# A second level of Strassen in the gate and value products of three of four segments

## The chip, the cores and the metric

The kernel runs on one core of a Trainium2 chip. The metric is device time in microseconds of one execution. Before the change the median was 796.1 us (794.5 to 797.4, three runs). Engines are named as the profile names them: PE is TensorE's matmuls, PEld its weight loads, DVE is VectorE, ACT ScalarE, POOL GpSimd, SPq the sequencer that issues most DMAs.

## The reference

A recurrent retention layer (batch 4, 8 heads, 768 positions, head size 64), whose output is turned into 3072 rows of 512, goes into a gated feed-forward block with 1536 hidden units. q, k, v and the output are fp32; the three weights arrive as fp64, and the kernel turns them into fp32 in segment 1, so all products are fp32.

```python
for t in range(S):
    state = gamma * state + outer(k[t], v[t])      # per head
    y[t] = scale * q[t] @ state
x = y.transpose(0, 2, 1, 3).reshape(3072, 512)
g = x @ w_gate
out = (g * sigmoid(g) * (x @ w_val)) @ w_out
```

## The kernel before

The 3072 rows are worked on in four segments. A segment has three stages: retention in chunks of 128 positions; **up**, the gate and value products for twelve blocks of hidden units; **down**, the product with `w_out` for three row tiles, between whose products the next segment's retention is slipped in. Up and down each use one level of Strassen-Winograd: seven products in place of eight. One block of up:

```python
def up(s, f, convert):
    ...
    def product(o, slot, a, start=True, stop=True):
        for k in range(KH):                        # KH = 2
            nc.tensor.matmul(o, w[:, slot, k], a[:, k], ...)   # 128 x 384
    product(x, B11, a_up(0, 0))
    p1 = tmp("p1", 2); nc.scalar.copy(p1, x)
    product(wb, T1, s1)
    p5 = tmp("p5", 1); nc.scalar.copy(p5, wb)
    product(x, T2, s2, start=False)                # accumulates onto x
    u2 = tmp("u2", 1); nc.scalar.copy(u2, x)
    product(wb, B22, s4, start=False)
    tt(hT[:, f, 0], wb, u2, op=add)                # VectorE
    ...                                            # three more products
    def muls():                                    # a block later
        tt(hT[:, f, 0], hT[:, f, 0], c11, op=mul)
        tt(hT[:, f, 1], hT[:, f, 1], sg, op=mul)
```

The seven operand blocks of a weight (four blocks and three differences) are made in segment 1 and kept in HBM for the later segments. In down, VectorE also makes four sums of the hidden activations per row tile (`sum_h`, 768 elements a partition).

## Time and profile before

I cut the span at the first and last matmul of each stage. In the last column stands the time in which PE neither streams nor overlaps, counted as steps between matmul starts that are over 0.15 us longer than the columns need.

| Stage | us | PE gaps, us |
|---|---|---|
| retention of segment 1 | 37.1 | (waits for its first loads) |
| up 1 | 130.4 | 21 |
| down 1 | 80.8 | 2.2 |
| up 2, up 3, up 4 | 108.4 each | 0 |
| down 2 | 78.4 | 0 |
| down 3 | 79.3 | 0.7 |
| down 4 | 54.2 | 0 |

### The profile page before, as it was taken

What the parts mean: (1) busy time and instruction counts of PE and PEld (TensorE: products, weight loads), DVE (VectorE), ACT (ScalarE), POOL (GpSimd) and SP (SyncE); (2) the same over time, 40 slices, a digit from 0 to 9 for tenths busy, and PEclk for the clock granted to TensorE, in tenths of its full rate; (3) what the DMA queues carried; (4) which work ended last, traced back from release to release, by engine and by line L of the source; (5) the groups of instructions that cost most, each with busy time, mean ns of one, the idle gap of its engine ahead of it and who ended that gap; (6) DMA issues with size and microseconds to landing.
All of it is one profiled execution on the core that took longest, in us unless ns stands there. A gap on an engine that the chain in (4) does not pass through costs nothing.

```text
span 794.6 us, 8792 instructions
## 1 busy us (share of the span) xinstructions
PE 758.9 (96%) x3440; PEld 532.4 (67%) x3440; DVE 333.4 (42%) x524; ACT 202.4 (25%) x422; POOL 138.2 (17%) x102
## 2 busy tenths in 40 slices
PE   5889888989999999999999999999999999999997
PEld 4755454557888555557888655556888755555886
DVE  2778888885241232225441322225433222223520
ACT  2374454411211222221122222322111122322100
POOL 3665766732110000100211000001211000000000
PEclk9899999999999999999999999999999999999999
DMA  9856667331550223500532223320254023310010
GB/s 328 287 199 232 203 220 250 148 120 54 186 195 31 93 92 99 192 0 28 199 118 108 73 93 113 128 97 14 67 212 159 27 93 113 119 47 0 1 54 26
DMA packets 40840, 95.73 MB, mean 120 GB/s; under 512 B 3680, under 2 KB 15968, under 8 KB 40800
## 3 DMA queue, kind: packets, MB, share of 16 engines
q1 hardware_dynamic: 37344, 88.89, 32.1%
q10 hardware_dynamic: 3456, 6.29, 2.3%
q8 instruction: 27, 0.44, 0.2%
q14 instruction: 13, 0.11, 0.0%
HBM read 77.86 MB, written 17.30 MB: 120 GB/s over the span
## 4 chain that ended last, share of the span: by engine, by line
PE 77%; DVE 3%; issue 0%; ACT 0%; DVEq 0%; ACTq 0%
PE x L349 24%; PE dx L417 15%; PE w L349 12%; PE dw L417 7%; PE z L349 6%; PE dz L417 4%; PE y L296 2%; PE s L246 2%; PE y L292 2%; PE st L274 2%; DVE hs L407 1%; DVE hT L390 0%; DVE a L251 0%; DVE hT L372 0%; DVE wot L201 0%
## 5 line engine op out<-in xcount | busy, mean ns | idle before, releaser
L349 PE MATMUL x<-xT,wt 128*128 128x384 f32 x384 | 136.3, 497 | 13.9 <-DVE hT L372 13.9
L349 PE MATMUL x<-xs,wt 128*128 128x384 f32 x384 | 139.8, 487 | 1.2 <-ACT u L368 1.2
L349 PE MATMUL w<-xs,wt 128*128 128x384 f32 x384 | 139.6, 486 | 0.9 <-DVE xs L334 0.9
L349 PEld LDWEIGHTS x<-xT,wt 128*128 128x128 f32 x384 | 73.8, 194 | 67.6 <-issue 20.8
L370 DVE TENSOR_TENSOR hT<-w,u 128x384 f32<-128x384 f32 x48 | 26.7, 557 | 214.0 <-PE w L349 213.1
L349 PEld LDWEIGHTS x<-xs,wt 128*128 128x128 f32 x384 | 72.7, 190 | 53.2 <-ACT u L368 3.3
L349 PEld LDWEIGHTS w<-xs,wt 128*128 128x128 f32 x384 | 73.0, 190 | 52.4 <-DVE xs L334 1.6
L257 POOL TENSOR_TENSOR kn<-kn,tab 128x512 f32<-128x512 f32 x20 | 25.2, 1261 | 330.4 <-DMA kn<-in_k_n_dram 330.4
L359 ACT COPY p<-x 128x384 f32<-128x384 f32 x48 | 23.0, 479 | 226.2 <-PE x L349 226.1
L349 PE MATMUL z<-xT,wt 128*128 128x384 f32 x192 | 69.8, 486 | 0.0
L417 PE MATMUL dw<-wot,hs 128*128 128x256 f32 x288 | 67.3, 383 | 0.0
L417 PE MATMUL dx<-wot,hs 128*128 128x256 f32 x288 | 67.0, 382 | 0.0
L417 PE MATMUL dx<-wot,hT 128*128 128x256 f32 x288 | 66.4, 381 | 0.0
L417 PEld LDWEIGHTS dw<-wot,hs 128*128 128x128 f32 x288 | 53.7, 190 | 8.7 <-issue 1.5
L417 PEld LDWEIGHTS dx<-wot,hT 128*128 128x128 f32 x288 | 53.7, 190 | 8.7 <-issue 0.9
L417 PEld LDWEIGHTS dx<-wot,hs 128*128 128x128 f32 x288 | 53.4, 190 | 7.7
L349 PEld LDWEIGHTS z<-xT,wt 128*128 128x128 f32 x192 | 36.5, 190 | 25.4
L299 ACT COPY xT<-y 128x512 f32<-128x512 f32 x24 | 14.1, 587 | 149.7 <-PE y L296 149.7
L251 DVE TENSOR_TENSOR a<-s,tab 128x512 f32<-128x512 f32 x48 | 30.9, 684 | 44.8 <-PE s L246 44.8
L281 DVE TENSOR_TENSOR state<-state,st 64x256 f32<-64x256 f32 x32 | 13.4, 419 | 79.8 <-PE st L274 77.1
L246 PE MATMUL s<-qt,kt 64*128 64x128 f32 x384 | 30.7, 298 | 12.8 <-DMA qt<-in_q_t_dram 10.5
L260 POOL TENSOR_TENSOR qt<-qt,tab 128x512 f32<-128x512 f32 x20 | 26.6, 1331 | 91.2 <-PE s L246 56.3
(58 smaller groups left out, 774.0 us busy)
## 6 DMA issues: line engine op xcount, KB each, us to landing
wt<-wstore SPq DMA_DIRECT2D x36, 896.0 KB, 4.6
wstore<-wt SPq DMA_DIRECT2D x12, 896.0 KB, 4.4
kt<-in_k_t_dram SPq DMA_DIRECT2D x24, 256.0 KB, 4.8
qt<-in_q_t_dram SPq DMA_DIRECT2D x24, 256.0 KB, 3.3
vn<-in_v_n_dram SPq DMA_DIRECT2D x24, 256.0 KB, 4.8
kn<-in_k_n_dram SPq DMA_DIRECT2D x24, 256.0 KB, 5.1
raw_up<-in_w_val_dram SPq DMA_DIRECT2D x24, 256.0 KB, 3.1
raw_up<-in_w_gate_dram SPq DMA_DIRECT2D x12, 512.0 KB, 5.0
```

The source lines that it names most:

```text
L246: nc.tensor.matmul(sp[i][:, ts(n, P)], kt[r, n], qt[r, n], start=True, stop=True, skip_group_check=True)
L251: nc.vector.tensor_tensor(t, pairs(sp[i]), mask[:, i], op=ALU.mult)
L257: nc.gpsimd.tensor_tensor(kd, kd, kdec[:, :, None].to_broadcast([P, H, D]), op=ALU.mult)
L260: nc.gpsimd.tensor_tensor(qt, qt, qdec, op=ALU.mult)
L274: nc.tensor.matmul(st[:, ts(n, P)], kd[:, ts(n, P)], vn[:, ts(n, P)], start=(n == 0), stop=True, skip_group_check=True)
L292: nc.tensor.matmul(y[:, ts(n, P)], prev[:, n], qd[:, n], start=(n == 0), stop=False, skip_group_check=True)
L296: nc.tensor.matmul(y[ds(D * i, D), ts(n, P)], vn[:, ts(2 * n + i, D)], a[i][:, n], start=(ci == 0 and n == 0), stop=True, skip_group_check ...
L299: nc.scalar.copy(xT[:, :, c // NCK % 2, ts(ci % L, P)], pairs(y))
L349: nc.tensor.matmul(o, w[:, slot, k], a[:, k], start=(start and k == 0), stop=(stop and k == KH - 1), skip_group_check=True)
L359: nc.scalar.copy(p1, x)
L370: tt(hT[:, f, 0], wb, u2, op=add)
L417: nc.tensor.matmul(o, a[:, k], wot[k][:, slot], start=(start and k == 0), stop=(k == FH - 1), skip_group_check=True)
```

## The change

Up of segments 2 to 4 gets a second level. Each of the seven products of the first level becomes a unit of seven products over a third of the hidden blocks (four of twelve), 21 units a segment, each product two fp32 matmuls of 192 columns. Two units run interleaved, so that one unit's evacuations pass beside the other's products. The unit's sums of x and of weights, the recombination in SBUF and the gates are spread over VectorE, ScalarE and GpSimd by an event list with hand-set times; one unit of that time is one product, 0.65 us. Weights of a unit are summed once (13 units in down 1, 8 in up 2) and kept in HBM. All places in SBUF and PSUM are fixed by hand, and down begins with the first product of two row tiles. Core of the diff:

```diff
-        for f in range(NF):
-            if s and f + 2 < NF:
-                kept_wt(s, f + 2)
-            up(s, f, convert if s == 0 else lambda f, part: None)
+    for f in range(NF):
+        up(f, convert)                       # segment 1 only
...
+        def stage(n):                        # one unit
+            ...
+            at(base, product, x, U11, a[:, 0, 0], True)
+            at(base + 2, product, wb, U1, sums[:, 0], True)
+            at(base + 4, product, x, U2, sums[:, 1], False)
+            ...                              # 6: U22, 8: U3, 10: U21, 12: U4
+                at(base + 2.6, pool, diagonal(c), t, diagonal(old), op=add)
+                at(base + 4.5, tt, c12, x, cell(old, 0, 1), op=add)
+                at(base + 12.5, tt, c21, x, cell(old, 1, 0), op=add)
+            at(base + 6.5, tt, c12, wb, c12, op=add)
+            at(base + 8.5, tt, c22, x, c22, op=add)
+            at(base + 10.5, tt, c11, z, c11, op=add)
+            if p in (6, 7):
+                by_block(9.5, 13.5, lambda r: pool(to[:, r], u2[:, r], p5[:, r], op=add))
+            elif p == 3:
+                by_block(10.7, 13.7, lambda r: tt(h0[:, r], h0[:, r], p1[:, r], op=mul))
...
+            if m < NU and m not in prepared:
+                for when, k in ((2.2, 0), (4.8, 1), (6.8, 2)):
+                    at(base + when, lambda k=k: sums_u(m)[k]())
...
+        if u == 0:
+            first(1)                         # early product of the second tile
```

In the list, `tt` is VectorE, `pool` GpSimd, `copy` and `silu` ScalarE; unit n has base 7n.

## The prediction

> **What bounds the kernel now.** I read the page first: TensorE is busy nearly throughout, at a full granted clock after the first tenth.
>
> ```profile
> PE 758.9 (96%) x3440; PEld 532.4 (67%) x3440; DVE 333.4 (42%) x524; ACT 202.4 (25%) x422; POOL 138.2 (17%) x102
> ...
> PEclk9899999999999999999999999999999999999999
> ```
>
> Busy matmul time alone proves little, so I cut the span by stage. The chain of waits gives the borders: gate and value ("up") of segment 1 end at 171 us, then come the output product with the next segment's retention ("down"), up 2 (253 to 361.5), down 2, up 3 (440 to 548), down 3, up 4 (627.6 to 736), down 4. Columns: stretch, its length, then busy us (instructions) per engine, clock, DMA share, GB/s.
>
> ```profile
> 52.00:171.00 119.00, 103.89 (x306) 58.62 (x305) 99.18 (x117) 54.27 (x82) 71.61 (x46) 0.97 0.61 210
> ...
> 253.00:361.50 108.50, 108.50 (x338) 63.95 (x338) 29.37 (x58) 26.98 (x60) 2.44 (x2) 1.00 0.26 92
> 361.50:440.00 78.50, 78.50 (x526) 67.46 (x525) 32.59 (x55) 14.04 (x40) 9.72 (x8) 1.00 0.33 115
> ```
>
> In up 2, and equally in up 3 and up 4, PE never stops, while VectorE works 29 us and GpSimd 2 us of 108.5. Is the PE stream itself as short as it can be? The chain in order of time gives the spacing (start, length, piece, instructions):
>
> ```profile
> 357.68 1.29 PE x L349 x4
> 358.97 1.29 PE z L349 x4
> 360.26 1.29 PE x L349 x4
> 361.55 2.59 PE dx L417 x12
> ```
>
> Four recorded matmuls of 384 columns take 1.29 us, 322.5 ns each; twelve of 256 columns take 2.59 us, 215.8 ns. Each fp32 matmul is recorded as two instructions. The slope is (322.5 - 215.8)/128 = 0.833 ns per column, the fixed part 2.5 ns. The clock is full and the cost is almost purely columns: only fewer columns shorten up 2 to 4.
>
> Segment 1 is different: 119 us, of which 13.9 us (the page's first row of groups, five waits) are of this kind:
>
> ```profile
> 70.98 2.39 POOL L190 TENSOR_TENSOR wt<-wt,raw_up 128x1024 int32<-128x1024 int32 x1 [4.33 <-DVE wt L188]
> 71.14 0.55 DVE L372 TENSOR_TENSOR hT<-x,p 128x384 f32<-128x384 f32 x1
> 71.61 2.18 DVE L389 TENSOR_TENSOR hT<-hT,c 128x384 f32<-128x384 f32 x1
> 71.81 2.23 PEld L349 LDWEIGHTS x<-xT,wt 128*128 128x128 f32 x8 [2.56 <-issue]
> 71.84 2.82 PE L349 MATMUL x<-xT,wt 128*128 128x384 f32 x8 [1.98 <-DVE hT L372]
> ```
>
> L389 has two SBUF inputs and lasts 2.18 us instead of its usual 0.55, until GpSimd's instruction is over. L372, with one input in PSUM, beside the same GpSimd instruction, keeps its 0.55. This will matter below.
>
> **What the Trainium skill says.** "TensorE: Matmul & The Clock Gate", section "Back-to-back issue gap", gives N/2.4 + 2.5 ns a matmul; my fit is that with two passes per recorded instruction (2 x 384/2.4 + 2.5 = 322.5), so the trace agrees. The same page, "LDWEIGHTS", puts a load of 128 columns at 128/1.2 = 107 ns. The state matmuls of 128 columns agree: eight in 1.05 us, whose last takes 0.275, so (1.05 - 0.275)/7 = 111 ns a step with a fresh load before each. Weight loads thus do not bind at 192 columns. "SBUF — State Buffer", "Who interferes with whom", says that a VectorE instruction with two SBUF inputs and a GpSimd instruction that reads SBUF exclude each other for a whole instruction: the lines above show it (2.18 against 0.55 us). "VectorE: DVE Perf Modes", the errata section, gives (N+151)/0.96 ns for an fp32 tensor_tensor: 557 ns at 384 and 957 at 768; this trace has 558 and 951 to 959, so I use it for new sizes.
>
> **The change part by part.**
>
> 1. Columns removed. Up 2 to 4 hold 12 blocks x 7 products x 2 matmuls x 3 = 504 matmuls of 384 columns; after, 21 units x 7 x 2 x 3 = 882 of 192. Recorded twice: 1008 x 322.5 ns = 325.1 us against 1764 x 162.5 ns (2 x 192/2.4 + 2.5, estimate from the fit) = 286.7. That is 38.4 us off PE's stream, 12.8 per segment, all on the path. The lost 1/8 of the columns is the second Strassen level; the 2.5 ns paid 756 times more is 1.9 us, included.
>
> 2. Edges. Down now begins with the first products of two tiles, 5.2 us of PE work that needs no new sums, and retention runs ahead so that the sums of the next up are ready. Before, PE waited about 2.2 us at 178 and 0.7 us at 554 for VectorE. I take off 2 us.
>
> 3. New work in up. A product now takes 4 x 162.5 = 0.65 us, a unit 7 of them, 4.55 us. VectorE evacuates three to five 384-element cells a unit (31 per seven units at 0.557 = 17.3 us) plus four 768-element multiplies (3.8): 21 us of 31.9, against 29 of 108.5 before. GpSimd gets nine 768-element adds per seven units; from 1.26 us at 512 elements and 2.39 at 1024 I estimate 1.83 each, 16.5 us of 31.9. Neither is full on average. But evacuations have slack of two other products: a PSUM bank is wanted back 1.95 us after its product ends, minus 0.2 latency and 0.56 of work leaves some 1.2 us. The multiplies have two SBUF inputs and share the time with GpSimd's adds. Following the queue from unit 3 to unit 7 with these durations, GpSimd runs back to back for about 16 us, and the first multiply of the sixth unit becomes ready within some 0.5 us of the start of GpSimd's next add. If GpSimd is first, the multiply and all evacuations behind it slip by 1.8 us and PE stalls about 1.2 us; if VectorE is first, nothing is lost. I count half: 0.6 us x 9 groups = 5 us.
>
> 4. Weight sums. Each unit needs three more subtractions (0.69 + 0.42 + 0.42 = 1.5 us, two SBUF inputs). Thirteen units are prepared in down 1 (20 us more VectorE, beside some 35 of 82), eight in up 2, on VectorE already two thirds full and exposed to the same lock: about 0.5 us each, 4 us.
>
> 5. DMA. Units are 896 KB and there are 21 per segment instead of 12: 19 MB in about 95 us, 200 GB/s; a 7 KB packet took 0.27 us, and 16 engines at that rate are over 400 GB/s, and loads run six units ahead. Down 1 is tighter: 13 loads of 0.5 MB, 13 stores of 0.9 MB, chunks and output are some 24 MB in 80 us, 300 GB/s, in one issue queue where a store waits for VectorE. Retention's chunks, now wanted sometimes one product (2.6 us) after issue against 3.3 to 4.8 us to landing, wait there: 4 us in down 1, 1 us in down 2 and 3 together.
>
> Sum: 796 - 38.4 - 2 + 5 + 4 + 5 = 770. I shade this to 767, because the event offsets (10.7, 13.7, 9.7) look placed to dodge collisions like that of part 3.
>
> **The rivals.** (a) VectorE becomes the bound. For: 68% in up rising above 80% in up 2, in-order queue, little slack, the segment 1 lines above. Against: averages below one and mostly one-SBUF-input evacuations. If each unit lost 0.4 us, 63 units cost 25 us: about 783, "same". (b) Weight loads or a per-instruction cost bind at 192 columns. For: a recorded load lasts 190 ns, more than the 162.5 ns step. Against: 128-column matmuls already step at 111 ns with one load each; 190 is a latency. If it did bind, 1764 x 190 = 335 us, slower than before: about 808. (c) Down 1 chokes on DMA and the in-order issue queue. For: 300 GB/s against the page's highest slice of 328. Against: ring of six and early issue; it happens once. It would add 10 to 15 us: about 778. (d) PE stays dense everywhere: 796 - 40 = 756, the floor.
>
> **Range and chances.** Floor 756; part 3 to 5 at double their estimate give 784. I predict 767 us, range 755 to 784. Faster by over 2% (under about 780) fails only if two of the costs come out double: 0.85; within 2% 0.13; slower 0.02, for rival (b).
>
> **What would show it.** Right: matmuls of 128x192 at 0.65 us per four, up 2 to 4 near 97 to 102 us each, up 3 and 4 shorter than up 2; waits of PE named after VectorE, beside L564 multiplies much longer than 0.96 us while GpSimd runs; up 1 still about 119 us. Wrong: up 3 and 4 at 108 us or more with PE still dense (rival b), VectorE near 100% there (a), PE waiting for chunks in down 1 for over 8 us (c). A lower granted clock, from PE gaps, would break the sum altogether.

## More of the kernel before

Busy time by stretch, from the windows view of the kernel before (stretch, length, then busy us and instructions of PE, PEld, DVE, ACT and POOL; PE clock, DMA share, GB/s). The rows are down 1, up 3, down 3 and up 4:

```profile
172.21:253.03 80.82, 78.93 (x526) 67.99 (x525) 33.91 (x56) 12.92 (x35) 12.21 (x9) 1.00 0.32 111
...
439.76:548.12 108.36, 108.36 (x337) 63.84 (x336) 29.92 (x60) 26.86 (x60) 1.41 (x1) 1.00 0.26 92
548.12:627.45 79.33, 78.93 (x526) 68.00 (x525) 32.79 (x55) 12.65 (x35) 12.45 (x9) 1.00 0.33 114
627.45:735.81 108.36, 108.36 (x338) 63.84 (x337) 29.37 (x58) 26.87 (x60) 0.00 (x0) 1.00 0.21 73
```

In up 3 and 4 PE's busy time is the stretch itself and VectorE, ScalarE and GpSimd each have over 70% of it to spare. That spare time is what the change wants to turn into fewer columns.

## The result, and the profile after

The changed kernel takes 787.8 us (786.3 to 788.9, four runs) against 796.2 us for the kernel before in the same rounds: 0.989, with a 95% interval of 0.987 to 0.992. Ratios are the mean time of one kernel's runs over that of the other's of the same rounds, so not quite the ratio of the medians. The prediction was 767 us with a range of 755 to 784, so the time lies outside the range and counts as the same at 2%.

The page of the changed kernel has more work on each engine except PE's matmuls:

```profile
PE 731.1 (93%) x4196; PEld 630.0 (80%) x4196; DVE 493.5 (63%) x782; ACT 224.7 (29%) x440; POOL 288.9 (37%) x183
...
L525 PE MATMUL bank<-loadp,ring 128*128 128x192 f32 x720 | 141.0, 327 | 2.2 <-ACT midp L490 2.2
```

The windows view of it, from down 1 to up 4, same columns as before:

```profile
172.82:260.29 87.47, 80.64 (x526) 69.34 (x525) 59.94 (x112) 12.72 (x35) 12.24 (x9) 0.98 0.71 257
260.29:361.68 101.39, 97.73 (x590) 95.30 (x589) 75.78 (x129) 33.79 (x66) 54.40 (x29) 1.00 0.60 210
361.68:441.21 79.53, 78.93 (x526) 67.68 (x526) 40.67 (x75) 14.58 (x39) 10.86 (x9) 1.00 0.38 136
441.21:543.13 101.92, 97.42 (x590) 95.36 (x589) 63.31 (x104) 33.98 (x66) 50.19 (x28) 1.00 0.48 162
543.13:626.49 83.36, 80.68 (x526) 69.21 (x526) 43.11 (x75) 13.00 (x35) 12.40 (x9) 0.98 0.37 130
626.49:728.42 101.93, 97.42 (x590) 95.36 (x589) 63.30 (x104) 33.98 (x66) 48.50 (x27) 1.00 0.42 141
```

Set against the table of before: up 2 to 4 gain 7.0, 6.4 and 6.4 us; down 1 to 3 lose 6.6, 1.2 and 4.0. The sum is -8.0 us, and the spans differ by 794.6 - 786.8 = 7.8. So there are two questions: why up gains 19.8 us and not 38.4, and why down loses 11.8.

**Up.** 588 recorded matmuls at 162.5 ns are 95.6 us; the stretches are 101.4 to 101.9. The timeline of up 3, at the first group's sixth unit:

```profile
470.11 1.81 POOL L490 TENSOR_TENSOR iop<-hsp,iop 128x768 f32<-128x768 f32 x1
...
470.29 2.45 DVE L564 TENSOR_TENSOR hT<-hT,midp 128x768 f32<-128x768 f32 x1
...
471.57 0.81 PE L525 MATMUL bank<-xT,ring 128*128 128x192 f32 x4
472.67 0.54 DVE L490 TENSOR_TENSOR iop<-bank,iop 128x384 f32<-128x384 f32 x1
473.13 0.54 DVE L490 TENSOR_TENSOR hT<-bank,hT 128x384 f32<-128x384 f32 x1
...
473.26 0.92 PE L525 MATMUL bank<-hsp,ring 128*128 128x192 f32 x4 [0.88 <-DVE iop L490]
```

GpSimd starts an add at 470.11; 0.18 us later VectorE starts the gate multiply, which has two SBUF inputs and lasts 2.45 us instead of 0.95. The evacuation that PE's next product waits for stands behind it, and comes at 472.67. PE loses 1.05 us, and 0.33 more a little later, because ScalarE may not overwrite p1 until the second multiply, now late too, has read it. The last group, which has no second unit beside it, loses 1.69 and 0.86. The same 0.18 us separate the two starts in all six groups of up 3 and up 4, and the multiply lasts 2.43 to 2.45 us in all six. In up 2, where weight sums shift the starts, the three groups differ: the multiply takes 2.09, 1.38 and 0.95 us, the last when it starts 0.15 us before GpSimd.

The groups of VectorE's multiplies in the changed kernel show the difference in the mean (busy us, then mean ns of one):

```profile
L564 DVE TENSOR_TENSOR hT<-hT,midp 128x768 f32<-128x768 f32 x18 | 28.0, 1558 | 0.0
...
L567 DVE TENSOR_TENSOR hT<-hT,iop 128x768 f32<-128x768 f32 x18 | 17.1, 950 | 0.1
```

L567 is the same operation at times when GpSimd rests.

**Down 1.** Two gaps carry it, 2.6 us from 205.0 and 4.2 us from 213.7. For the second, the DMA queue's own timeline (start, length, what, count):

```profile
206.57 4.12 SPq L174 DMA_DIRECT2D unitt<-ring  x2
210.75 0.42 SPq L112 DMA_DIRECT2D loadp<-in_k_t_dram  x1
211.28 0.84 SPq L112 DMA_DIRECT2D loadp<-in_q_t_dram  x1
```

The second of two stores of summed units stands in the queue until VectorE has done its sum (the sum ended at 210.34), and the chunk loads behind it are issued only then. PE wants q at 213.7 and starts on it at 217.9; from issue to landing the load of q took 6.5 us here, against 2.4 to 3.4 in down 1 before the change.

**Down 3.** VectorE's timeline and PE's:

```profile
547.77 1.91 DVE L596 TENSOR_TENSOR hsp<-hT,hsp 128x768 f32<-128x768 f32 x1
548.82 1.75 POOL L320 TENSOR_TENSOR loadp<-loadp,tab 128x512 f32<-128x512 f32 x1
549.60 1.79 DVE L596 TENSOR_TENSOR hsp<-hT 128x768 f32<-128x768 f32 x1
...
551.32 1.27 DVE L314 TENSOR_TENSOR midp<-bank,tab 128x512 f32<-128x512 f32 x2
552.04 0.29 PEld L308 LDWEIGHTS bank<-loadp 64*128 64x128 f32 x2 [2.69 <-DVE midp L314]
...
553.73 4.54 PE L607 MATMUL bank<-wot,hsp 128*128 128x256 f32 x12
```

Two of the sums of the hidden activations last 1.8 to 1.9 us beside GpSimd, the mask L314 stands behind them, and PE waits 2.45 us for the score bank. Then twelve matmuls that take 2.86 us at full clock (e3 below) take 4.54. The window of that moment shows why: the granted clock (third figure from the end) is half.

```profile
553.80:557.20 3.40, 3.40 (x8) 2.76 (x9) 1.12 (x2) 0.00 (x0) 1.27 (x1) 0.50 0.00 0
```

Before the change the four sums began 1.4 us into down 3, not 2.7, and one of them was held, not two; the gap was 0.45 us.

### The profile page after: what moved, and what is told of

Read it like the earlier page. It is cut to its first block, busy times and chain, and to the rows that moved or that the text cites. A ratio compares the mean times of both kernels' runs of the same rounds, so it can differ in the third digit from the quotient of the medians.

```text
span 786.8 us, 10948 instructions
## 1 busy us (share of the span) xinstructions
PE 731.1 (93%) x4196; PEld 630.0 (80%) x4196; DVE 493.5 (63%) x782; ACT 224.7 (29%) x440; POOL 288.9 (37%) x183
## 4 chain that ended last, share of the span: by engine, by line
PE 62%; DVE 11%; issue 3%; ACT 1%; DMA 1%; POOL 0%; ACTq 0%; SPq 0%; DVEq 0%
PE bank L525 30%; PE bank L607 23%; DVE hsp L596 3%; PE bank L359 2%; PE bank L308 2%; PE bank L355 2%; DVE iop L490 2%; PE bank L337 1%; PE bank L413 1%; DVE hT L564 1%; DMA loadp<-in_q_t_dram 1%; DVE hT L490 1%; DVE midp L314 1%; ACT midp L490 1%; DVE ring L169 1%
## 5 line engine op out<-in xcount | busy, mean ns | idle before, releaser
L525 PE MATMUL bank<-loadp,ring 128*128 128x192 f32 x720 | 141.0, 327 | 2.2 <-ACT midp L490 2.2
L607 PE MATMUL bank<-wot,hsp 128*128 128x256 f32 x576 | 132.2, 385 | 0.0
L525 PEld LDWEIGHTS bank<-loadp,ring 128*128 128x128 f32 x720 | 120.4, 190 | 4.9 <-ACT midp L490 4.9
L607 PEld LDWEIGHTS bank<-wot,hsp 128*128 128x128 f32 x576 | 108.7, 192 | 15.9 <-issue 0.7
L490 DVE TENSOR_TENSOR iop<-bank,iop 128x384 f32<-128x384 f32 x144 | 79.4, 553 | 61.3 <-PE bank L525 59.3
L607 PE MATMUL bank<-wot,hT 128*128 128x256 f32 x432 | 98.7, 382 | 2.7 <-DVE iop L643 2.7
L607 PEld LDWEIGHTS bank<-wot,hT 128*128 128x128 f32 x432 | 80.9, 190 | 15.3 <-DVE iop L643 3.2
L525 PE MATMUL bank<-xs,ring 128*128 128x192 f32 x432 | 87.9, 326 | 0.0
L525 PEld LDWEIGHTS bank<-xs,ring 128*128 128x128 f32 x432 | 73.2, 190 | 0.0
L413 PEld LDWEIGHTS bank<-xs,ring 128*128 128x128 f32 x192 | 36.3, 191 | 28.9 <-ACT iop L432 1.9
L413 PEld LDWEIGHTS bank<-xT,ring 128*128 128x128 f32 x144 | 29.0, 205 | 36.2 <-issue 20.1
L525 PEld LDWEIGHTS bank<-xT,ring 128*128 128x128 f32 x324 | 54.8, 190 | 3.4 <-DVE iop L490 3.2
```

What stands on the lines that cost most here:

```text
L413: nc.tensor.matmul(o, w[:, slot, k], a[:, k], start=(start and k == 0), stop=(stop and k == KH - 1), skip_group_check=True)
L490: events.append((t, len(events), lambda: fn(*args, **kw)))
L525: nc.tensor.matmul(o[:, h], w[:, h, slot], rhs, start=(start and h == 0), stop=True, skip_group_check=True)
L607: nc.tensor.matmul(o, a[:, k], wot[k][:, slot], start=(start and k == 0), stop=(k == FH - 1), skip_group_check=True)
```

## The experiments

The theory for up: the hold of the multiply by GpSimd. Its rival: VectorE at 62 to 75% simply cannot turn the banks round in time. For down: VectorE's queue and the issue queue behind it, against full DMA engines. "Change" below is the changed kernel, 787.8 us, as measured above; each run was timed beside the kernel before (796.4 to 796.7 us). Stage lengths come from one profile each. One difference between profiles is nobody's edit: up 1 takes 130.7 us or, with 3.4 us at half clock at 161 to 164 us, about 132.4 (e2, e3, e5, e6, e8 and e10 drew the longer one). So compare stages, and medians of the whole kernel, but not the whole spans of two profiles.

**e1, the multiply earlier.**

```diff
-                by_block(10.7, 13.7, lambda r: tt(h0[:, r], h0[:, r], p1[:, r], op=mul))
+                by_block(8.7, 13.7, lambda r: tt(h0[:, r], h0[:, r], p1[:, r], op=mul))
```

> One event is moved: the first gate multiply of each group's sixth unit (two SBUF inputs, line L564) is put right behind that unit's c22 evacuation instead of behind c11. Theory (the multiply starts 0.18 us after a GpSimd add of 1.81 us, is held until it ends, and holds four evacuations and PE behind it): placed earlier it meets the end of the add before, gets in between two adds, and the 1.0 to 1.7 us gap of each group goes, with the 0.3 to 0.9 us gap behind it. PE gaps over 0.15 us in the up stretches of segments 3 and 4 fall from 6.4 us to 2 or less each, kernel 787.8 to 775-778 us. Rival (VectorE's load alone is too much for the 1.95 us bank turn-round): the same work in another order still stalls PE somewhere else in the group, gaps stay at 5 to 6 us, kernel within 2 us of 787.8.

Measured 779.7 us, ratio 0.980 (0.976 to 0.983, so unclear at 2%), a little short of the 775 to 778 expected. Up 3 and up 4 fall from 101.9 to 98.4 and 97.7 us. VectorE, then GpSimd, at the same place in up 3 of this run:

```profile
468.84 1.68 DVE L564 TENSOR_TENSOR hT<-hT,midp 128x768 f32<-128x768 f32 x1
470.44 0.55 DVE L490 TENSOR_TENSOR hT<-bank,hT 128x384 f32<-128x384 f32 x1
```

```profile
467.88 1.82 POOL L560 TENSOR_TENSOR hT<-iop 128x768 f32<-128x768 f32 x1
469.78 2.42 POOL L490 TENSOR_TENSOR iop<-hsp,iop 128x768 f32<-128x768 f32 x1
```

The multiply waits for the end of the add before it and then goes ahead of the next, which now takes 2.42 us instead of 1.81. GpSimd has that time. PE gaps are 2.3 us in up 3 and 1.5 in up 4, and inside the groups there are none: what is left is the start and the end of the stretch. The rival's 5 to 6 us did not come. In up 2 it went the other way (103.0 us from 101.4): a weight sum behind the multiply took over its collision, with gaps of 2.17 and 0.66 us. Up 2 to 4 together are 6.1 us shorter; the rest of the 8 us is not the edit's own. Down 1 lies before any edited instruction, and its 4.2 us gap was 1.1 in this profile: it varies from run to run. Down 3 kept its gap of 2.45 us, but the half clock did not follow it this time (81.7 us from 83.4).

**e2, no GpSimd in up.**

```diff
-        tt, copy, pool = nc.vector.tensor_tensor, nc.scalar.copy, nc.gpsimd.tensor_tensor
+        tt, copy, pool = nc.vector.tensor_tensor, nc.scalar.copy, nc.vector.tensor_tensor
```

> All nine adds per group of the second level go from GpSimd to VectorE, so that up has no GpSimd work at all (weight sums and multiplies on VectorE can then never be held). Theory (the hold by GpSimd costs the time): no VectorE multiply is longer than 0.97 us; but 9 x 0.96 = 8.6 us are added to 21 us of VectorE per 31.9 us of matmuls, so the queue runs late anyway; up of segments 3 and 4 at 100 to 106 us, about equal to 101.9. Rival (VectorE's load is what stalls PE already at 21 us): 30 us of 31.9 makes it far worse, up at 110 us or more and the kernel over 805 us.

Measured 786.6 us, 0.988 (0.985 to 0.990). The windows view of its up 3:

```profile
446.62:546.37 99.75, 97.42 (x589) 95.35 (x588) 79.45 (x131) 34.15 (x66) 1.04 (x1) 1.00 0.49 165
```

VectorE is busy 79 us of 99.8, 16 more than in the change, and up 3 is 2.2 us shorter. L564 averages 0.947 us there. This is the clearest evidence against the rival in up 3 and 4: more load without the hold is faster than less load with it. The 110 us or more that the rival asked for are far off. In up 2, with weight sums on top, it is slower (103.8), so VectorE is not free of limits, and the whole kernel gains only about 1 us.

**e3, two hidden sums behind the first masks.**

```diff
-        for n in (1, 2, 4, 3):
+        for n in (1, 2):
             sum_h(n, 0)
+        later_h = [4, 3]
...
+            if later_h and (k > 1 or not nxt):
+                sum_h(later_h.pop(0), 0)
```

> At the start of each down, two of the four 768-element sums of the hidden activations are put on VectorE behind the masking of the first score tiles, instead of all four in front. Theory (in down 3 the masking waits behind four sums, two of which GpSimd holds for 0.9 us each; PE idles 2.45 us and its clock is halved for some 2 us afterwards): the gap of 2.45 us at the second score product and the slow product behind it go, down 3 falls from 83.4 to about 79.5 us, down 1 and 2 by 0.5 us each, kernel about 783 us. Rival (down 3 is longer because of the unit loads of the next up in the same queue): down 3 stays at 83 us.

Measured 783.6 us, 0.983 (0.981 to 0.985). Down 3 is 78.7 us from 83.4, down 2 78.4 from 79.5, down 1 87.2 from 87.5. The gap is gone and with it the half clock behind it. The first masks and the twelve matmuls, in this run:

```profile
547.19 1.28 DVE L314 TENSOR_TENSOR midp<-bank,tab 128x512 f32<-128x512 f32 x2
550.31 2.86 PE L607 MATMUL bank<-wot,hsp 128*128 128x256 f32 x12
```

The rival (unit loads) falls.

**e5, stores issued one product later.**

```diff
-            nc.sync.dma_start(out=unit_t[n], in_=w)
+            defer.append(lambda: nc.sync.dma_start(out=unit_t[n], in_=w))
...
+            while stores:                    # next step, behind its chunk loads
+                stores.pop(0)()
```

> In down 1 each store of a summed unit is issued one product later, behind that step's chunk loads, so the in-order issue queue does not wait for VectorE's sums in front of a chunk load. Theory (the 4.2 us gap at 213 us is the issue queue standing behind a store whose sum VectorE had not finished): the gap falls under 1 us, down 1 from 87.5 to about 83.5 us, kernel about 784 us. Rival (the DMA engines themselves are full in down 1, with some 300 GB/s asked for): the chunk still lands late, the gap keeps over 3 us.

Measured 785.5 us, 0.986 (0.984 to 0.988). The store now goes out at once, and the load of q behind it is issued 34.7 us into down 1 instead of 38.5:

```profile
207.93 0.33 SPq L177 DMA_DIRECT2D unitt<-ring  x1
208.30 0.43 SPq L112 DMA_DIRECT2D loadp<-in_k_t_dram  x1
208.84 0.83 SPq L112 DMA_DIRECT2D loadp<-in_q_t_dram  x1
```

Down 1 falls from 87.5 to 81.8 us, and the 4.2 us gap is gone with the same loads and stores in the same stretch. So the order in the queue was the cause and not the amount; e6 agrees, which moves 149 GB/s in down 1 where the change moves 257 and keeps a gap of 3.1 us. The median falls by only 2.3 us: the gap varies (1.1 to 4.2 us in the six profiles without this edit), and this profile drew the longer up 1.

**e7, the fourth hidden sum behind the evacuation of x** (with e5's edit).

```diff
-        more(1, 2, 4)
+        more(1, 2)
...
-        more(3)
+        more(4, 3)
```

> The later-store version of down 1 with one more edit: of the next tile's sums of hidden activations, the fourth goes behind the evacuation that frees the x bank, so one 0.96 us sum less stands in front of it. Theory (the 2.56 us gap at 206 us is VectorE's queue: three such sums, four sums of x held by GpSimd's two decay multiplies, two weight sums, then the evacuation that PE waits for): the gap shrinks by about 1 us to 1.6, down 1 from 81.8 to 80.8, kernel about 784.5. Rival (the evacuation itself waits for PE or a bank): no change.

Measured 783.2 us, 0.983 (0.982 to 0.985). The gap at 205 us is 1.50 us instead of 2.56 and down 1 80.7 us: one sum less in front is one sum's time less, as the theory has it.

**e4, the early product undone.**

```diff
-        if u == 0:
-            first(1)
```

> Undoes one part of the change: the first product of the second row tile goes back into its own tile, so that down begins with one product without new sums (2.6 us) instead of two (5.2 us). The prediction's step 2 held that the second product removes waits: without it, after the longer tail of the second level (two 768-element gates and multiplies), PE should then wait for the first sum, some 1 to 3 us in each of the four downs, and the kernel be 3 to 8 us slower than the change, 791 to 796. Rival (retention's own matmuls and masks cover the tail, and the early product only brings the masks forward into the sums): down 3 loses its 2.45 us gap and the kernel is the same or up to 3 us faster.

Measured 783.6 us, 0.984 (0.982 to 0.985). Neither expectation holds. The edit is faster, so the product does not save what step 2 of the prediction gave it; but down 3 keeps its 2.46 us gap, so the rival is wrong too. The gain is in down 1, 81.4 us instead of 87.5: its two large gaps are 0.85 and 1.26. Why the early product lengthens down 1 was not tested by itself. Only the last down, without retention, shows the wait that I had feared, 1.09 us. Up 3 took 100.7 us here, and shows what the tie decides: in its second group GpSimd's add came later, VectorE started 0.18 us before it, the multiply took 0.95 us, and PE's gap was 0.21 us instead of 1.03.

**e6, seven units' weight sums moved from down 1 to up 2.**

```diff
-    to_sum = list(range(RING + 1, NU, 2)) + resident
+    to_sum = list(resident)
```

> The weight sums of seven units are moved from down 1 into the up of segment 2, where fifteen instead of eight units are then summed (4.5 us of VectorE more per seven units; the seven loads, sums and stores leave down 1). Theory (down 1 is long because stores and sums of the units stand in the issue queue and on VectorE): down 1 falls from 87.5 to 80-82 us; up of segment 2, with two-input sums now in every unit that meet GpSimd's adds, rises from 101.4 to 105-110 us; together 784 to 790. Rival (VectorE has no slack left in up at 68%): up of segment 2 rises to 115 us or more, the kernel over 793.

Measured 794.0 us, 0.996 (0.995 to 0.998). Up 2 rises to 108.3 us, seven units for 6.9 us, as expected. Some 3.2 of these are slow clock: gaps of 2.46 and 2.44 us are each followed by 3.4 us at half clock. Down 1 falls by only 0.9, to 86.6, with gaps of 1.5 and 3.1 us left. The first half of the expectation holds; the second fails: fewer stores do not help while one stands in the wrong place.

**e8, the mends together** (e1 in segments 3 and 4 only, e3, e5, e7).

> The mends together: the early multiply in segments 3 and 4 alone (segment 2 keeps the place of the change, where its weight sums make the early one worse), the sums of hidden activations behind the first masks, the later stores, the later fourth sum. If the gains add: down 1 at 80.5 (from 87.5), up of segment 2 at 101.4, down 2 at 78.4, up of 3 and 4 at 98 (from 101.9 each), down 3 at 78.7 (from 83.4): 787.8 - 7 - 1.1 - 7.8 - 4.7 = 767 us, which is where the prediction stood. If they are the same microseconds counted twice, or waits move on to the next place, it stays above 774.

Measured 768.7 us (767.2 to 770.0), 0.965 (0.964 to 0.967). Down 1 79.9, up 2 101.3, down 2 78.4, up 3 98.4, down 3 78.4, up 4 97.7. The gains add.

**e9, e8 with the early multiply in all segments and up 2's colliding weight sums moved.**

```diff
-                for when, k in ((2.2, 0), (4.8, 1), (6.8, 2)):
+                for when, k in (((2.2, 0), (4.8, 1), (6.8, 2)) if i < 6 else
+                                ((9.2, 0), (10.8, 1), (11.8, 2))):
```

> The mends together, with the early multiply in segment 2 as well, and there the three weight sums that fall into the sixth-to-seventh unit put behind GpSimd's last add of the group. Theory (in the early-multiply run segment 2 lost 2.17 and 0.66 us because a weight sum took the place of the multiply in front of that add): both go, up of segment 2 falls from 101.3 to about 98.5-99.5 us and the kernel from 768.7 to about 766.5. Rival (with weight sums VectorE is simply late in segment 2): up stays at 101 us or more, the kernel at 768 or above.

Measured 766.4 us (765.8 to 768.4), 0.962 (0.961 to 0.964). Its windows from up 2 to up 4:

```profile
252.75:353.17 100.42, 97.70 (x590) 95.31 (x589) 76.79 (x129) 33.78 (x66) 55.18 (x29) 1.00 0.60 212
...
431.54:529.97 98.43, 96.67 (x590) 95.41 (x589) 61.74 (x104) 34.07 (x66) 51.33 (x28) 1.00 0.50 167
...
608.34:706.01 97.67, 96.67 (x589) 95.41 (x588) 61.01 (x104) 33.97 (x66) 50.33 (x27) 1.00 0.43 147
```

Up 2 is 100.4 us, 0.9 less, where the expectation had 1.8 to 2.8. The median is 2.3 us below e8's, but 1.7 us of the difference between the two profiles lie in up 1, where e8 drew the half clock. This version beats both kernels, by 30 us the one before and by 21 us the change, with the same work on each engine.

**e10, e9 with the early product kept in the last down alone.**

> As the run before it, and the early product of the second row tile is kept in the last down alone. Undone everywhere it had shortened down 1 by 6 us, which I had not foreseen, and lengthened the last down by 1.2. Theory (the early product moves the next tile's sums of hidden activations onto the same products as the sums of x and the chunk loads, so VectorE's queue is long just where the x bank and the stores wait): the gap of 1.57 us left in down 1 goes, down 1 at 78.5 us, kernel 1 to 1.5 us below the run before it. Rival (the effect in down 1 was the store order alone, which is mended): no difference, within 0.5 us.

Measured 767.2 us (765.4 to 767.5), 0.963 (0.961 to 0.964), no difference from e9 (766.4). In down 1 the gap is 0.85 instead of 1.57 us and the stage 79.3 instead of 79.9, where the theory had no gap and 78.5: right in direction, and too small to show in the time. So nearly all of what e4 gained in down 1 is also gained by the mends already in e9.

## Why the prediction was wrong

**Step 1, the stream: right.** 128 x 192 matmuls step at 162.5 ns wherever nothing waits, and the 38.4 us are there. Rival (b), a bound by weight loads, did not occur: PEld rose to 95 of 102 us busy without slowing PE. One reading says less than it seems to: by the prediction's own fit, two passes of 128 columns take 109 ns, so the step of 111 ns shows that a load takes no longer than that, not that it takes 107.

**Step 3, up's new work: the mechanism was right, the term mis-sized.** I had found the very multiply and the very add, and that it would be decided by less than 0.5 us. Then "I count half: 0.6 us x 9 groups = 5 us". That is the step that failed. The list of events repeats, so the order of two starts is not a coin: it fell against VectorE by 0.18 us in all six groups of up 3 and 4. e1, which moves the multiply out of its way, gives 3.5 us for the three groups of up 3 and 4.3 for those of up 4: 1.3 us a group, not 0.6. I also left out the late second multiply, which keeps p1 (0.33 us), the last group, which has no second unit beside it (1.69), and waits at the ends of a stretch that no mend removed (0.36 at the start, 0.86 or more at the end). With step 4's 4 us for weight sums, up's stalls were put at 9 us; they measure 305.2 - 286.7 = 18.5, the length of up 2 to 4 less 1764 x 162.5 ns. In e9, with the starts mended, 9.8 of these are left. Step 4's own size depends on the schedule: in the change up 2, with its eight units' sums, is no longer than up 3 and 4 without, but once the multiply is early it is 4.6 us longer than up 3 (e1), or 2.0 with the sums moved as well (e9).

**Step 2, edges: the sign was wrong.** "I take off 2 us" for the early product. e4 shows it worth 1.1 us in the last down and a loss of 6.1 us in down 1, of which 0.5 is left once stores and sums are mended (e10). The gap that it should have closed in down 3 grew from 0.45 to 2.45 us, because the hidden sums start later behind the longer tail of up and meet GpSimd's two decay multiplies; in e3 it is gone. I knew the hold and looked for it only in up. The half clock after that gap, worth 1.7 us in twelve matmuls, was named among the signs of being wrong but costed in no step. Nor was VectorE's queue in down 1, the gap of 2.6 us (e7).

**Step 5, DMA: right in kind.** The issue queue where "a store waits for VectorE" was named, with 4 us for down 1; e5 measures 5.7 in its profile. The 300 GB/s that I set beside it were no trouble: 257 GB/s in the change, 281 in e9 without that gap.

**In sum:** 796.2 - 38.4 + 18.5 (up) + 11.8 (down) = 788.1, measured 787.8. I had 9 and 3 for the two stalls, and then took 3 us off "because the event offsets [...] look placed to dodge collisions", which no line of the profile supported. The rival closest to the outcome, (a), put 0.4 us on each unit; 18.5 us over 63 units is 0.3. Its reason, VectorE's load, is refuted by e2 for up 3 and 4.

## What to carry to other kernels

In a hand-set schedule that repeats, a near tie is not a fair coin: in up 3 and 4 of the six profiles that leave this part alone (the change, e3 to e7) it fell the same way in 35 of 36 groups. Work out or measure who starts first, and do not take an average. When work moves to GpSimd or to VectorE, list every VectorE instruction with two SBUF inputs in front of a PSUM evacuation, in the neighbouring stages too, and place it where GpSimd has just ended. In an in-order issue queue, put a store that waits for compute behind the loads that something else is waiting for.

## What the Trainium skill lacked or had wrong

- "SBUF — State Buffer", section "Who interferes with whom", has the hold right (2.45 us for a 0.95 us multiply) and says that the one to issue first gets the pair. It lacks the hand-over: in e1 a waiting VectorE multiply goes between two back-to-back GpSimd adds (the second lasts 2.42 instead of 1.81 us). No L564 multiply of the change or e1 waited longer than the rest of the GpSimd instruction that it met.
- "TensorE: Matmul & The Clock Gate", section "Why this matters for your kernels", advises against PE gaps over some 3 us. Shorter gaps can be enough, and need not be: that of 2.45 us in down 3 was followed by 3.4 us at half clock in the change, e2, e4, e5, e6 and e7, but not in e1, and that of 2.56 us in down 1 of the change was not.
- The same page, section "Back-to-back issue gap": its N/2.4 + 2.5 ns fits at 192, 256 and 384 columns, and at 128 within 3 ns, if a recorded fp32 matmul is counted as two passes with the 2.5 ns once. The "sustained" figures of that section for streams of load and matmul (81 ns at 128 columns, 131 at 512) are not seen: 128 columns take 56 ns a pass here, with a load before each, and 384 already take 161.
